# The diagonal superblock of each couple by eight block products in place of seven

## The chip, the core and the metric

The kernel runs on one core of one Trainium2 chip. The metric is the device time of one launch in microseconds; lower is better. The kernel before was run three times: 1091.76, 1091.03 and 1094.78 us, median 1091.76 us.

## What is computed

```python
scores = scale * np.matmul(z, z.transpose(0, 2, 1))      # scale = 1/S, z: (8, 3072, 64)
attn = np.maximum(scores, 0.0) ** 2
out = np.matmul(attn, v)                                 # v: (8, 3072, 256)
x = (u * out).reshape(8 * 3072, 256)
h1 = x @ w1
h2 = x @ w2                                              # w1, w2: (256, 1024)
out = np.maximum(h1, h2) @ w_out                         # w_out: (1024, 256)
```

Inputs and the output are float32; the kernel works in bfloat16 with float32 sums. The scores are symmetric, since both sides are z.

## The kernel before, in words

**Tiling.** A batch has 3072 rows: 24 tiles of 128, 6 groups of 4 tiles (512 rows), 3 couples of 2 groups. `A[b, g, blk]` is a score block of 512 keys by 512 queries, already through relu and square. It fills one of 27 SBUF slots of 128x2048 bf16. Only blocks with `blk >= g` are computed, each in two "pairs" (`score_pair`, L188): two matmuls over 64 rows (L202) into two of the four PSUM buffers of `mm_psum`, a relu on ScalarE into one of three `r_sb` buffers (L215), a square on VectorE into the slot (L223, or L221 for the blocks on the diagonal, of which the triangle alone is computed and the rest is turned over by DMA, L226). A block off the diagonal is turned by one DMA from SyncE into a second slot (`mirror`, L249, DMA at L251), which gives `A[b, blk, g]`.

**Slots.** `free` is a list; a new `Block` takes its first entry, and `release` appends. A block that is to be mirrored has two uses: the mirror is one (it releases when the DMA is issued, not when it has landed), the products are the other. A slot thus can come back into `free` as soon as a mirror is issued, and what is then written there waits until that DMA has read it.

**Couples.** Batch 0 is done by plain loops, its last couple by `plain_steps`. From batch 1 on, for each couple (b, c) the rows of A that belong to it are three superblocks of 2x2 blocks, one for each couple `o` of keys; o = c is the superblock on the diagonal. With v cut into 2x2 parts, A times v is done by seven products of blocks in place of eight (Winograd's form). It needs sums of blocks S1, S2, S3 (`prepare`, L307 to L330) and S4 (L760), each one VectorE instruction over 128x2048, and sums of parts of v (`combine_v`, L155). S1 and S2 take a slot each; S3 and S4 are written over A21 and A12.

**Two kinds of stage alternate on TensorE.** In an A stage the products of one couple are issued (L837): every step is two matmuls of 64 contraction rows, one in each half of the array, into different PSUM banks (`ORDER`, `BANK`); 84 steps for a couple. A product is done half in each lane; where it changes lane, a GpSimd no-op stands between the halves. Between the steps, at places worked out by hand, stand the 14 score pairs of later blocks, the mirrors, the adds of finished products into `h` (L742) and the DMA issues for u, z and v. In an F stage (`second`, L669) the two groups of the couple before go through the feed-forward (`ff`, L420): max(h1, h2) is done as relu(x(w1-w2)) plus x w2, so 16 matmuls of 512 columns (L425), eight relus from PSUM on ScalarE (L432), and 40 matmuls of 256 columns (L440, L448); then a copy (L456) and the DMA out from ScalarE's queue (L457). During an F stage VectorE runs a list of tasks: the four products with u ("gates", L409) of the couple just finished, and `prepared` for the couple that comes next. A hook lets six tasks of the list into the instruction stream in each `ff` (after the first and the fourth relu, and after each of the four output tiles), the rest come after both.

**When mirrors are issued in the kernel before.** `urgent` (L238) lets a mirror go at once if its block will be overwritten by S3 or S4 (g + blk odd); the others wait until the couple in whose products they are used, and are issued there when more than `KEEP` slots are free (5, from step 37 on 2).

**Where pairs are issued.** `at_step` spreads 14 pairs over an A stage; `asked` holds one back while three squares are outstanding or no slot is free.

Of the kernel before, what the change touches and what calls it, by code (L numbers as in the profile page):

```python
# [11 lines left out]
def kernel(  # L12
# [10 lines left out]
    nc = tc.nc  # L23
    fp32 = mybir.dt.float32
    bf16 = mybir.dt.bfloat16
# [10 lines left out]
    G = 4  # L36
# [6 lines left out]
    NSLOTS = 27  # L43
    AFTER = mybir.DependencyInfo(mybir.DependencyClass.Sync, mybir.DependencyReason.DATA)
    PLAIN = 4
    KEEP = 5, 2
    c2 = float((1.0 / S) * (1.0 / S))

    consts = ctx.enter_context(tc.tile_pool(name="consts", bufs=1))
# [105 lines left out]
    def combine_v(b, piece):  # L155
        w = vp[b, piece]
        b11, b12 = w[:, 0:G, 0:P], w[:, 0:G, P:D]
        b21, b22 = w[:, G : 2 * G, 0:P], w[:, G : 2 * G, P:D]
        t = tpool.tile([P, 3, G, P], bf16, name="vt")
        t1, t2, t3, t4 = vt[b, piece] = b12, t[:, 0], t[:, 1], t[:, 2]  # L160
        return [
            lambda: nc.vector.tensor_sub(t3, b22, b12),
            lambda: nc.vector.tensor_sub(t1, b12, b11),
            lambda: nc.vector.tensor_sub(t2, b22, t1),
            lambda: nc.vector.tensor_sub(t4, b21, t2),
        ]


# [66 lines left out]

        return finish

    def urgent(b, g, blk):  # L238
        return b == 0 or (g + blk) % 2

    def mirror_ready(now=None, keep=0):
        for only in (True, False):
            for x in list(to_mirror):
                if urgent(*x) if only else (x[0], x[1] // 2) == now:
                    if len(free) > (0 if only else keep):
                        to_mirror.remove(x)
                        mirror(*x)

    def mirror(b, g, blk):  # L249
        t = Block(turned=True)  # L250
# [43 lines left out]

    def alike(*blocks):
        if len({x.turned for x in blocks}) == 1:
            return [x.ap for x in blocks]
        return [  # L300
            x.ap.rearrange("p (k j r) -> p j k r", k=G, r=P)
            if x.turned
            else x.ap.rearrange("p (j k r) -> p j k r", k=G, r=P)
            for x in blocks
        ]

    def prepare(b, c):  # L307
        forms, tasks = {}, []
        for o in (c, *(o for o in range(NC) if o != c)):
            f = {  # L310
                f"A{q + 1}{k + 1}": A[b, 2 * c + q, 2 * o + k]
                for q in range(2)
                for k in range(2)
            }
            forms[o] = f

            def s1(f=f):
                f["S1"] = Block(f["A22"].turned)
                nc.vector.tensor_add(*alike(f["S1"], f["A21"], f["A22"]))  # L319

            def s2(f=f):
                f["S2"] = Block(f["A22"].turned)
                nc.vector.tensor_sub(*alike(f["S2"], f["S1"], f["A11"]))  # L323

            def s3(f=f):
                f["S3"] = f["A21"]
                nc.vector.tensor_sub(*alike(f["S3"], f["A11"], f["A21"]))  # L327

            tasks.append([s1, s2, s3])
        return forms, tasks  # L330

    ORDER = (
        (("P1", "P7", "P6", "X11"), ("P6", "X11", "P1", "P7")),
        (("X21", "X12", "P5"), ("P5", "X12b", "X21")),
    )
    BANK = {"P1": 0, "P6": 1, "P7": 2, "X11": 3, "X21": 0, "P5": 1, "X12": 2, "X12b": 3}
    PLAIN_BANK = {"D11": 0, "D12": 1, "D21": 2, "D22": 3}
    FORM = {
        "P1": ("A11", 11),
        "P6": ("S2", 1),  # L340
        "P7": ("S3", 2),
# [1 line left out]
        "P5": ("S1", 0),  # L343
        "X21": ("A22", 3),
        "X12": ("S4", 22),
        "X12b": ("S4", 22),
    }

    def product(b, c, forms, name):
        form, side = FORM[name]  # L350
        steps = []
        for o in forms:
            for j in range(G):
                if side >= 10:
                    k, dc = side // 10 - 1, side % 10 - 1
                    w = lambda o=o, j=j, k=k, dc=dc: v_at(b, (2 * o + k) * G + j, dc)
                else:
                    w = lambda o=o, j=j, side=side: vt[b, o][side][:, j, :]
                steps.append((name, w, lambda o=o, form=form: forms[o][form], j))
        return steps  # L360

    PLAIN_LANES = (("D11", "D12", "D21", "D22"), ("D21", "D22", "D11", "D12"))

# [56 lines left out]
    def ff(b, g, xT, last=False, hook=lambda *at: None):  # L420
        g_sb = gpool.tile([P, KF, GW], bf16, name="g_sb")
        for nb in range(KF):
            d_ps = mm_psum.tile([P, GW], fp32, name="d_ps", tag="mm")
            for kc in range(KD):
                nc.tensor.matmul(  # L425
                    d_ps,
                    w15_sb[:, kc, ts(nb, P)],
                    xT[:, kc, :],
                    start=(kc == 0),
                    stop=(kc == KD - 1),  # L430
                )
            nc.scalar.activation(g_sb[:, nb, :], d_ps, AF.Relu)  # L432
            hook(1, nb)
        dst = by_tile(out[ds(b * S, S), :])[:, ds(g * G, G), :]
        for t0 in range(0, G, 2):
            o_ps = mm_psum.tile([P, 2, D], fp32, name="o_ps", tag="mm")
            o_sb = opool.tile([P, 2, D], fp32, name="o_sb")
            for t in range(2):
                for dc in range(KD):
                    nc.tensor.matmul(  # L440
                        o_ps[:, t, :],
                        xT[:, dc, ts(t0 + t, P)],
                        W2o_sb[:, dc, :],
                        start=(dc == 0),
                        stop=False,
                    )
                for nb in range(KF):
                    nc.tensor.matmul(  # L448
                        o_ps[:, t, :],
                        g_sb[:, nb, ts(t0 + t, P)],  # L450
                        w_out_sb[:, nb, :],
                        start=False,
                        stop=(nb == KF - 1),
                    )
                hook(2, t0 + t)
            nc.scalar.copy(o_sb, o_ps)  # L456
            nc.scalar.dma_start(out=dst[:, ds(t0, 2), :], in_=o_sb)  # L457
# [77 lines left out]
    with tc.manual_schedule():  # L535
# [150 lines left out]
        def prepared(i, gates):  # L686

            b, c = couples[i]
            for o in range(NC):
# [2 lines left out]
                    for q in (2 * c, 2 * c + 1)  # L692
                    for k in (2 * o, 2 * o + 1)
                ), (i, done)
            for x in list(to_mirror):
                if x[0] == b and x[2] // 2 == c:
                    to_mirror.remove(x)
                    mirror(*x)
            if not b:
                return {}, list(gates)  # L700
            tasks = []
            for o in reversed(range(NC)):
                if (b, o) not in vt:
                    tasks += combine_v(b, o)
            forms, sums = prepare(b, c)
            first, *others = [x[:2] for x in sums]
            tasks = list(gates) + first + tasks + sum(others, [])
            return forms, tasks + [x[2] for x in sums]

        b, g = groups[PLAIN - 1]  # L710
        sums = drain(acc, range(KD))
# [4 lines left out]
        for i in range(PLAIN // 2, len(couples)):  # L716
# [13 lines left out]
            for f in forms.values():  # L730
                for name, n in (("A11", 1), ("A12", 2), ("A21", 1), ("A22", 1), ("S1", 1)):
                    f[name].quota = 2 * G * n
            if not b:
                for q in (q1, q2):
                    for k in range(NG):
                        A[b, q, k].quota = 4 * G
            for pair in steps:
                for x in pair:
                    left[x[0]] = left.get(x[0], 0) + 1
# [25 lines left out]
            def c11():  # L765
                add(h["1"], h["1"], h["x"])

            def after_x12():
                add(h["U2"], h["U2"], acc["X12"])
                add(h["U2"], h["U2"], acc["X12b"])  # L770

            def after_p5():
                h["V"] = new_h()
                add(h["V"], h["U3"], acc["P5"])
                add(h["U2"], h["U2"], acc["P5"])

            def after_x21():
                add(h["U3"], h["U3"], acc["X21"])

            def after_plain():  # L780
                for n, name in enumerate(("D11", "D12", "D21", "D22")):
                    h[name] = new_h()
                    copy = nc.vector.tensor_copy if n % 2 else nc.scalar.copy
                    copy(h[name], acc[name])

            events = {}
            f = list(forms.values())
            for n, do in () if not b else (
                (ends["P6"], after_p1),
                (ends["P6"], after_p6),  # L790
                (ends["P7"], after_p7),
                (ends["X11"], after_x11),
                (ends["X11"] - 7, lambda: s4(f[0])),
                (ends["X11"] - 3, lambda: s4(f[1])),
                (ends["X11"], lambda: s4(f[2])),
                (ends["X11"] + 18, c11),
                (ends["X12"], after_x12),
                (ends["P5"], after_p5),
                (ends["X21"], after_x21),
            ):  # L800
                events.setdefault(n, []).append(do)
# [15 lines left out]
                    if b or c == 2:  # L817
                        events.setdefault(n, []).append(do)

            asked = 0  # L820
            for s, pair in enumerate(steps):
                tick += 1
                flush(tick)
                mirror_ready((b, c), KEEP[s > 36])
                asked += len(at_step.get(s, ()))
                while asked and len(due) < 3 and (free or pairs[done][2] % 2):
                    emit_pair(wait=6)
                    asked -= 1
                for do in events.get(s, ()):
                    do()  # L830
                for half, (name, w, blk, j) in enumerate(pair):
# [20 lines left out]
                    a.quota -= 1  # L852
                    if not a.quota:
                        a.release()
            assert not asked, (i, asked)
            flush()
            for do in events.get(len(steps), ()):
                do()
# [47 lines left out]
```

## Time and profile before

| | |
|---|---|
| median of three runs | 1091.76 us |
| the profiled execution: its own time / its span | 1091.76 us / 1089.9 us |
| mean granted TensorE clock | 0.937 |
| busy: TensorE / VectorE / ScalarE | 966.8 / 720.1 / 612.9 us |
| DMA queue q1 (DMAs of SyncE, nearly all transposes), share of 16 engines | 48.8% |
| DMA queue q0 (loads, GpSimd) and q10 (stores) | 18.5% and 6.5% |
| A stage matmuls (L837) | 3720 |

The profile page shows one execution. "Busy" of a matmul row overlaps with its neighbours, since two halves of the array work side by side, so a mean duration there is no price of a step; the length of a stage is. The chain of work that ended last says what the end had to wait for. The table of waits says who was idle and what ended it. A table by stretches of time gives for each stretch its length, the busy time of each engine with the number of its instructions, the granted clock and the DMA share. The run is periodic from batch 1 (129.45 us) on: three A and three F stages for each batch.

### The profile page before, as it was taken

The page shows a single profiled execution, that of the slowest core. Times are in us where ns is not written, and L with a number is a line of the kernel's source. Part 1 is how long each engine was busy: PE and PEld are TensorE (multiplying, and loading weights), DVE is VectorE, ACT ScalarE, POOL GpSimd, SP SyncE. Part 2 cuts the span into 40 slices and gives each one's busy share as a digit, 9 for nine tenths or more (in the row PEclk, how much of TensorE's full clock was granted, in tenths as well). Part 3 has the DMA queues.
Part 4 walks back from the last instruction along what each step waited for, and adds up shares of the span by engine and source line. Part 5 has one row for each costly group of instructions (what it writes and reads, how often), then busy time and mean ns, then how long its engine had stood idle before and what let it go on. Part 6 is the DMA issues. An engine that isn't in the chain of part 4 may idle for free.

```text
span 1089.9 us, 19275 instructions
## 1 busy us (share of the span) xinstructions
PE 966.8 (89%) x7538; PEld 518.6 (48%) x7538; DVE 720.1 (66%) x1098; ACT 612.9 (56%) x1206; POOL 56.6 (5%) x111
## 2 busy tenths in 40 slices
PE   9989969799697996969969799697996979969998
PEld 4445525455253552535525445253552544525555
DVE  6844837679385794857938679475793867937740
ACT  7877635466464664637636476454663647644425
POOL 3000000000000000000000000000000000000000
PEclk9999978899898998989989899798998989989999
DMA  9999586956979469695686956869569795684701
GB/s 180 188 208 183 112 150 120 165 103 130 155 125 158 109 124 161 126 154 108 124 151 130 156 119 123 151 125 150 103 129 150 131 157 116 122 146 95 134 28 59
DMA packets 388652, 145.99 MB, mean 134 GB/s; under 512 B 361936, under 2 KB 365904, under 8 KB 388560
## 3 DMA queue, kind: packets, MB, share of 16 engines
q1 hardware_dynamic: 359328, 90.09, 48.8%
q0 software_dynamic: 15408, 29.50, 18.5%
q10 hardware_dynamic: 13824, 25.17, 6.5%
q8 instruction: 59, 0.97, 0.4%
q14 instruction: 33, 0.27, 0.1%
HBM read 59.77 MB, written 25.17 MB: 78 GB/s over the span
## 4 chain that ended last, share of the span: by engine, by line
PE 68%; ACT 15%; DMA 11%; DVE 2%; SPq 2%; issue 2%; ACTq 1%; DVEq 0%
PE acc L837 35%; PE o_ps L448 13%; ACT g_sb L432 12%; DMA blk<-blk 11%; PE d_ps L425 7%; PE s_ps L202 6%; PE acc L267 3%; PE o_ps L440 3%; ACT o_sb L456 1%; ACT r_sb L215 1%; DVE blk L223 1%; SPq L178 1%; SPq L251 1%; ACTq L457 1%; DVE blk L221 0%
## 5 line engine op out<-in xcount | busy, mean ns | idle before, releaser
L215 ACT ACTIVATE r_sb<-s_ps 128x512 bf16<-128x512 f32 (+3 forms) x664 | 329.4, 557 | 263.3 <-DVE blk L223 123.7
L837 PE MATMUL acc<-blk,v_sb 64*128 64x512 bf16 x2208 | 459.0, 381 | 0.0
L837 PE MATMUL acc<-blk,vt 64*128 64x512 bf16 x1512 | 373.3, 383 | 0.0
L223 DVE TENSOR_TENSOR blk<-r_sb 128x1024 bf16<-128x1024 bf16 x251 | 168.7, 688 | 172.9 <-DMA blk<-blk 104.9
L425 PE MATMUL d_ps<-xT,w_sb 128*128 128x512 bf16 x768 | 212.1, 422 | 61.1 <-ACT r_sb L215 57.5
L837 PEld LDWEIGHTS <-v_sb 64*128 64x128 bf16 x2208 | 177.9, 95 | 136.0 <-issue 7.3
L432 ACT ACTIVATE g_sb<-d_ps 128x512 bf16<-128x512 f32 x384 | 198.4, 624 | 37.5 <-PE d_ps L425 34.6
L448 PE MATMUL o_ps<-w_out_sb,g_sb 128*128 128x256 bf16 x1536 | 210.0, 274 | 6.5 <-ACT g_sb L432 5.6
L837 PEld LDWEIGHTS <-vt 64*128 64x128 bf16 x1512 | 141.3, 95 | 73.4 <-issue 8.8
L202 PE MATMUL s_ps<-zT 64*128 64x512 bf16 (+3 forms) x672 | 128.8, 361 | 49.0 <-ACT r_sb L215 47.7
L448 PEld LDWEIGHTS <-g_sb 128*128 128x128 bf16 x1536 | 151.1, 98 | 38.4 <-ACT g_sb L432 19.9
L425 PEld LDWEIGHTS <-w_sb 128*128 128x128 bf16 x768 | 78.9, 105 | 183.6 <-issue 132.2
L456 ACT COPY o_sb<-o_ps 128x512 f32<-128x512 f32 x96 | 56.2, 586 | 151.3 <-PE o_ps L448 147.1
L742 DVE TENSOR_TENSOR h_sb<-h_sb,acc 128x512 f32<-128x512 f32 x147 | 96.8, 682 | 42.6 <-ACT h_sb L746 35.4
L221 DVE TENSOR_TENSOR blk<-r_sb 128x512 bf16<-128x512 bf16 (+3 forms) x170 | 48.1, 321 | 109.2 <-DMA blk<-blk 62.7
L323 DVE TENSOR_TENSOR blk<-blk,blk 128x2048 bf16<-128x2048 bf16 x63 | 77.2, 1225 | 2.1
L319 DVE TENSOR_TENSOR blk<-blk,blk 128x2048 bf16<-128x2048 bf16 x63 | 76.7, 1217 | 2.3 <-DMA blk<-blk 2.3
L202 PEld LDWEIGHTS <-zT 64*128 64x128 bf16 x672 | 35.7, 94 | 88.8 <-issue 50.0
L761 DVE TENSOR_TENSOR blk<-blk,blk 128x2048 bf16<-128x2048 bf16 x63 | 76.5, 1217 | 0.0
L440 PE MATMUL o_ps<-W2o_sb,xT 128*128 128x256 bf16 x384 | 74.8, 277 | 0.0
L327 DVE TENSOR_TENSOR blk<-blk,blk 128x2048 bf16<-128x2048 bf16 x63 | 73.2, 1217 | 0.0
L409 DVE SCALAR_TENSOR_TENSOR xT<-h_sb,uT 128x512 bf16<-128x512 f32 x96 | 59.9, 682 | 0.0
(52 smaller groups left out, 295.9 us busy)
## 6 DMA issues: line engine op xcount, KB each, us to landing
out_dram<-o_sb ACTq DMA_DIRECT2D x96, 256.0 KB, 2.2
un<-in_u_dram POOLq DMA_DIRECT2D x48, 256.0 KB, 5.3
v_sb<-in_v_dram POOLq DMA_DIRECT2D x21, 512.0 KB, 6.3
blk<-blk SPq DMA_TRANSPOSE x246, 4.7
zn<-in_z_dram POOLq DMA_DIRECT2D x21, 128.0 KB, 3.9
v_sb<-in_v_dram POOLq DMA_DIRECT2D x6, 256.0 KB, 7.3
blk<-in_moe_w_dram POOLq DMA_DIRECT2D x2, 512.0 KB, 7.2
uT<-un SPq DMA_TRANSPOSE x48, 3.6
```

What stands on the lines that cost most here:

```text
L202: nc.tensor.matmul(s_ps[h][:, lo[h] :], zT[rows, z_at(b, blk * G + tiles[h]), :], zT[rows, q + lo[h] // P : q + G, :].rearrange("p t c -> ...
L215: nc.scalar.activation(o, s, AF.Relu)
L223: nc.vector.tensor_mul(a[:, k : k + 2, :], r, r)
L319: nc.vector.tensor_add(*alike(f["S1"], f["A21"], f["A22"]))
L323: nc.vector.tensor_sub(*alike(f["S2"], f["S1"], f["A11"]))
L425: nc.tensor.matmul(d_ps, w15_sb[:, kc, ts(nb, P)], xT[:, kc, :], start=(kc == 0), stop=(kc == KD - 1),)
L432: nc.scalar.activation(g_sb[:, nb, :], d_ps, AF.Relu)
L440: nc.tensor.matmul(o_ps[:, t, :], xT[:, dc, ts(t0 + t, P)], W2o_sb[:, dc, :], start=(dc == 0), stop=False,)
L448: nc.tensor.matmul(o_ps[:, t, :], g_sb[:, nb, ts(t0 + t, P)], w_out_sb[:, nb, :], start=False, stop=(nb == KF - 1),)
L742: nc.vector.tensor_add(out, a, b_)
L761: nc.vector.tensor_sub(f["A12"].ap, f["A12"].ap, f["S2"].ap)
L837: mm = nc.tensor.matmul(a.out(acc[name]), w()[rows], a.moving(rows, j), start=name not in opened, stop=left[name] == 0,)
```

## The change

The superblock on the diagonal is multiplied by plain products; the two others keep the seven. A couple's products are now: P1, P6, P7, P5 of 8 steps, X11, X12, X21 of 8 steps for the two superblocks off the diagonal and 8 for the own one, and a new D22 of 8: 88 steps in place of 84. The order of the products, their banks and their lanes change. S1 to S4 are formed for two superblocks, so a couple takes 4 slots for sums in place of 6. `combine_v` writes four parts into a tile of its own and is called for pieces other than the couple's own.

Mirrors go in the order in which their blocks are ready, as soon as any slot is free; `urgent`, `KEEP` and the mirrors at the head of `prepared` are gone. A pair is issued at its step, with no `asked`. In `ff`, three of the eight relus go to VectorE.

Over the whole kernel TensorE gets 3888 matmuls at L837 in place of 3720; VectorE 42 each of S1, S2, S3, S4 in place of 63, and 144 relus from PSUM; ScalarE 240 relus there in place of 384; `combine_v` stays at 84 instructions, and all loads, stores and transposes stay the same in number. The diff, cut to its core:

```diff
-        t = tpool.tile([P, 3, G, P], bf16, name="vt")
-        t1, t2, t3, t4 = vt[b, piece] = b12, t[:, 0], t[:, 1], t[:, 2]
+        t = tpool.tile([P, 4, G, P], bf16, name="vt")
...
-    def mirror_ready(now=None, keep=0):
-        for only in (True, False):
-            for x in list(to_mirror):
-                if urgent(*x) if only else (x[0], x[1] // 2) == now:
-                    if len(free) > (0 if only else keep):
-                        to_mirror.remove(x)
-                        mirror(*x)
+    def mirror_ready(keep=0):
+        while to_mirror and len(free) > keep:
+            mirror(*to_mirror.pop(0))
...
-        for o in (c, *(o for o in range(NC) if o != c)):
+        for o in range(NC):
+            if o == c:
+                continue
...
     ORDER = (
-        (("P1", "P7", "P6", "X11"), ("P6", "X11", "P1", "P7")),
-        (("X21", "X12", "P5"), ("P5", "X12b", "X21")),
+        (("P1", "P6", "P7", "X11"), ("X11", "P1", "P6", "P7")),
+        (("D22", "X12", "P5", "X21"), ("P5", "X21", "D22", "X12")),
     )
-    BANK = {"P1": 0, "P6": 1, "P7": 2, "X11": 3, "X21": 0, "P5": 1, "X12": 2, "X12b": 3}
+    BANK = {"P1": 0, "P6": 1, "P7": 2, "X11": 3, "D22": 0, "P5": 1, "X21": 2, "X12": 3}
...
+    OWN = {"X11": (0, 0), "X12": (0, 1), "X21": (1, 0), "D22": (1, 1)}
...
+        if name in OWN:
+            q, dc = OWN[name]
+            for k in range(2):
+                for j in range(G):
+                    own.append((
+                        name,
+                        lambda k=k, j=j, dc=dc: v_at(b, (2 * c + k) * G + j, dc),
+                        lambda k=k, q=q: A[b, 2 * c + q, 2 * c + k],
+                        j,
+                    ))
+        return own + off if name in ("X12", "X21") else off + own
...
-            nc.scalar.activation(g_sb[:, nb, :], d_ps, AF.Relu)
+            if nb in (2, 5, 7):
+                nc.vector.tensor_single_scalar(
+                    out=g_sb[:, nb, :], in_=d_ps, scalar=0.0, op=ALU.max
+                )
+            else:
+                nc.scalar.activation(g_sb[:, nb, :], d_ps, AF.Relu)
...
-            for x in list(to_mirror):
-                if x[0] == b and x[2] // 2 == c:
-                    to_mirror.remove(x)
-                    mirror(*x)
...
-            first, *others = [x[:2] for x in sums]
-            tasks = list(gates) + first + tasks + sum(others, [])
-            return forms, tasks + [x[2] for x in sums]
+            return forms, list(gates) + sums[:3] + tasks + sums[3:]
...
-                (ends["P6"], after_p1),
+                (ends["P1"], after_p1),
                 (ends["P6"], after_p6),
+                (ends["P6"] + 2, lambda: s4(f[0])),
                 (ends["P7"], after_p7),
                 (ends["X11"], after_x11),
-                (ends["X11"] - 7, lambda: s4(f[0])),
-                (ends["X11"] - 3, lambda: s4(f[1])),
-                (ends["X11"], lambda: s4(f[2])),
-                (ends["X11"] + 18, c11),
+                (ends["X11"] + 3, lambda: s4(f[1])),
+                (ends["X11"] + 7, c11),
+                (ends["D22"], after_d22),
+                (ends["P5"], after_p5),
                 (ends["X12"], after_x12),
-                (ends["P5"], after_p5),
                 (ends["X21"], after_x21),
...
-            asked = 0
             for s, pair in enumerate(steps):
                 tick += 1
                 flush(tick)
-                mirror_ready((b, c), KEEP[s > 36])
-                asked += len(at_step.get(s, ()))
-                while asked and len(due) < 3 and (free or pairs[done][2] % 2):
+                mirror_ready()
+                for _ in at_step.get(s, ()):
                     emit_pair(wait=6)
-                    asked -= 1
```

## The prediction, made before the changed kernel was run

> **What bounds the kernel now.** I read the chain of waits first, for what the end hangs on, then the table by stretches, for which stages are long, then the waits, for what makes them long, and last one such place in the timeline. The chain of the page:
>
> ```profile
> PE 68%; ACT 15%; DMA 11%; DVE 2%; SPq 2%; issue 2%; ACTq 1%; DVEq 0%
> ```
>
> TensorE carries it, but 11% is a DMA from slot to slot: a mirror. The table by stretches for batch 4 (start:end, length, busy PE, PEld, DVE, ACT, POOL, then clock, DMA share, GB/s), six stages A, F, A, F, A, F; the fifth and sixth are the third couple's:
>
> ```profile
> 537.64:567.97 30.33, 23.06 (x197) 10.54 (x197) 14.28 (x23) 14.13 (x29) 1.59 (x3) 0.90 0.71 126
> 567.97:589.05 21.08, 18.49 (x114) 11.24 (x114) 18.64 (x23) 11.11 (x21) 0.53 (x1) 0.91 0.60 126
> 589.05:609.67 20.62, 20.62 (x198) 10.49 (x197) 11.79 (x26) 12.70 (x29) 1.59 (x3) 1.00 0.98 154
> 609.67:634.58 24.91, 18.10 (x114) 11.04 (x112) 19.20 (x27) 11.10 (x21) 1.05 (x2) 0.86 1.00 164
> 634.58:655.84 21.26, 21.26 (x197) 9.48 (x197) 14.72 (x22) 16.49 (x31) 1.58 (x3) 1.00 0.54 103
> 655.84:672.74 16.90, 16.58 (x116) 10.69 (x114) 16.49 (x27) 9.81 (x19) 0.01 (x1) 1.00 0.69 136
> ```
>
> The last two are what a stage costs when nothing is missing: TensorE is busy throughout and the clock is 1.00. The first, second and fourth do the same matmuls in 9.1, 4.2 and 8.0 us more, TensorE idle for a part of it and at a lower clock. The waits name the cause (who waited on whom: us, times, longest):
>
> ```profile
> ACT r_sb L215 <- DVE blk L223: 123.7, 33, 9.2
> DVE blk L223 <- DMA blk<-blk: 104.9, 14, 9.6
> DVE blk L221 <- DMA blk<-blk: 62.7, 6, 11.9
> PE d_ps L425 <- ACT r_sb L215: 57.5, 13, 8.4
> PE s_ps L202 <- ACT r_sb L215: 47.7, 7, 7.4
> ```
>
> Bottom to top it is one chain: the square that writes a score block stands on VectorE until a mirror has read the slot; the three `r_sb` buffers fill; ScalarE stops; the PSUM buffers fill; TensorE stops, 20 times (14 + 6 squares wait, 13 + 7 stalls). The timeline of batch 4 shows one:
>
> ```profile
> 558.40 9.20 SPq L251 DMA_TRANSPOSE blk<-blk  x3
> 562.97 1.29 DVE L223 TENSOR_TENSOR blk<-r_sb 128x1024 bf16<-128x1024 bf16 x2 [9.52 <-DMA blk<-blk]
> 564.41 1.07 PE L202 MATMUL s_ps<-zT 64*128 64x512 bf16 x2 [7.27 <-ACT r_sb L215]
> ```
>
> **What the stalls cost.** Stages of all seven batches against the clean ones: first couple's A, 30.15, 29.76, 29.69, 30.33, 29.56, 30.42, 29.24, together 209.2, against 7 x 21.26: 60.3 us. The F behind it, 22.24, 20.89, 19.58, 21.08, 22.31, 20.89, 23.24, together 150.2, against 7 x 16.89: 32.0. The F behind the second couple's A in six batches, 25.05, 26.64, 27.91, 24.91, 27.18, 24.50, together 156.2, against 6 x 16.89: 54.9. Sum **147.2 us**. Of it 57.5 + 47.7 = 105.2 is TensorE's idle time; the other 42, some 2.1 for each stall, is work at a low clock right after, as a shorter stretch shows (same columns, clock 0.50):
>
> ```profile
> 564.00:568.00 4.00, 3.59 (x15) 1.12 (x15) 0.27 (x1) 1.82 (x4) 0.00 (x0) 0.50 1.15 208
> ```
>
> The Trainium skill (TensorE: Matmul & The Clock Gate, "What's actually happening") says that an idle window of about 3.4 us halves the clock until a busy one has passed; half of 3.4 is 1.7 a stall, 34 us for 20, so by that rule the sum would be 8 us smaller than by the rows.
>
> **Do the stalls go?** In before, a block with two uses whose products are done is released by its mirror; five mirrors are issued in steps 42 to 49 of the first couple's A, and the next blocks (steps 48 and 60) take just those slots. Followed through both programs as built: in before exactly 20 VectorE squares wait for a mirror issued 19, 26 or 40 matmuls earlier. In the changed one mirrors go one at a time, about 12 steps apart, while their blocks are still needed, so slots come free from the products or from S4 (on VectorE itself); no VectorE or ScalarE instruction of a stage stands within 90 matmuls of a mirror that it waits for. Two slots fewer for sums pay for the earlier mirrors. So all 20 go: **-147.2**, with an uncertainty that the rivals carry. Next in line is then TensorE's own work.
>
> **More products.** 4 steps more in each of 21 couples, 84 steps (168 matmuls). The clean A stage of 21.26 us has 84 steps and 14 score pairs: 98 places, 0.217 us each. 84 x 0.217 = **+18.2**, on the path in every A; nothing hides it, for TensorE is busy there throughout.
>
> **VectorE's sums.** 84 instructions of 128x2048 at 1.22 us (rows L319, L323, L327, L761), 102 us, leave VectorE. They lay beside TensorE's work; nothing by itself.
>
> **Three relus of eight.** 144 leave ScalarE (row L432, 0.624 us) and cost VectorE the row L213's 0.684, 98.5 us in all. A clean F has 2 x (16 x 0.223 + 40 x 0.109) = 15.9 us of matmuls (the chain has 16 of L425 in 3.57 us, 8 of L448 in 0.87), so about 1.0 of 16.9 is the wait for the last relus: the most that can be won is 1.0 x 24 F stages = 24 us. But VectorE is in order and 16.49 of 16.90 us busy in a clean F. Ahead of the last relu of the second `ff` now stand: two adds of the A stage 1.4, four gates (L409, 0.682) 2.7, S1 to S3 3.65, one task more 0.43 to 1.22, six relus 4.1: 12.3 to 13.1 us. TensorE wants it 8.6 (first `ff`) + 16 x 0.223 + 10 x 0.109 = 13.2 us in. So the relus arrive about in time; in the first `ff` adds, gates and relus (1.4 + 1.4 + 2.1 = 4.9, from about 0.4) end at 5.3, no better than ScalarE's 4.7 to 5.1 now. I take a fifth of the possible gain, **-5**. If all tasks had to end within F, VectorE would need 1.4 + 2.7 + 7.3 + 8 x 0.425 + 4.1 = 18.9 us, 2.0 more: +48. Ends kept: -24 and +48. A rule of the skill speaks against this edit (VectorE: DVE Perf Modes, "Specifications"): VectorE sits closer to SBUF, ScalarE to PSUM. The rows agree mildly, 0.684 against 0.597 (L215) and 0.624 (L432); by them the move adds 144 x 0.06 to 0.09, some 9 to 13 us, of busy time, which is not the path as long as F keeps its length.
>
> **Moved steps.** S2 and S3 of the second superblock end up after all other tasks: in the longest F (eight `combine_v`) VectorE ends about 19.5 us in, and step 12 of the next A, which needs it, is at 16.5 + 14 x 0.217 = 19.5. Banks are taken over after 8 steps (1.7 us) where it was 12: X21 needs the add of P7 (0.68, behind one square 0.69 and one S4 1.22) and X12 the copy of X11 (0.59, behind up to two relus, 1.2). Between 0 and 0.3 us a couple; I take 0.15 x 21, **+3**. The relays stand in GpSimd's queue behind the same loads as before. The transposes of u (steps 42, 48) now have three mirrors ahead of them in SyncE's queue in the third couple's A, which had at most one. q1's 48.8% is 532 us for 90.09 MB, so a mirror of 0.524 MB takes 3.1 us of all engines: 3 x 3.1, two halves for u, and loads of 7 (q0: 202 us for 29.5 MB, 1 MB here) make 19.5; the gates want u at about 23. Nothing.
>
> **Sum.** 1091.8 (the profiled execution's own time, 1.9 over its span, and equal to the median) - 147.2 + 18.2 - 5 + 3 = **961 us**.
>
> **Rivals.** *VectorE paces F*: the tasks and relus together bind, +48 in place of -5: 1014 us. For it: 16.49 of 16.90. Against: only part of the tasks stands ahead of a relu. *Half the stalls stay*, because mirrors that run on through every stage bring q1 late and something waits that I counted as free: 961 + 74 = 1035. For it: DMA time of 73.8% of 1090 us is 84% of 961, and the third couple's A has seven mirrors where three were issued. Against: no waiting instruction is near its mirror. *Slower*: in the third couple's A the transposes of u come so late that the first gate waits in F; a relu stands behind it on VectorE, TensorE behind that, and the clock falls. It decides when u is over 4 us late (23 - 19.5), and to pass 1091.8 it has to take 131 us, 18.7 in each of 7 batches or 5.5 in each F: such as 1110 us. Against: the clean A stage at 589.05 us carries a DMA share of 0.98 without a stall. *No effect*: the same count of stalls and relus that win back the 18 us: about 1092; the order as built speaks against it.
>
> **Chances.** 961 with all its terms (940 to 985) 0.74; VectorE paces F (985 to 1015) 0.12; half the stalls stay 0.07; slower 0.05; no change 0.02. The range takes the first two with the relus' ends: 935 (all of 24 won, 961 - 19, and a little) to 1012. A measurement tells 0.3% from no change: faster by more 0.93, within 0.02, slower 0.05.
>
> **What would show it.** Right: no line "DVE blk <- DMA blk<-blk" of any size; granted clock near 1.00; all A stages of 21.5 to 22.2 us, all F of 16 to 17.5. Wrong: an F over 18 with relus behind S tasks (first rival); a gate waiting on "DMA uT<-un" (slower); squares that wait for a mirror (half the stalls).

## The result and the profile after

The changed kernel takes **946.39 us** (median of four runs, 943.65 to 954.8; the kernel before beside it 1093.27, 1091.03 to 1096.02): a ratio of 0.867, 95% interval 0.861 to 0.873. 961 had been predicted, with a range of 935 to 1012. (In experiments 1, 6, 10 and 11 one of the four executions was over 1.5% longer than the fastest, at a lower clock; the medians here are of all four, the ratios and intervals leave that one out.) The profiled execution took 945.2 us, its span 943.4; the mean granted clock rose from 0.937 to 0.996.

The chain of work that ended last, on the page of the kernel after:

```profile
PE 91%; DVE 5%; ACT 1%; issue 1%; DMA 1%; SPq 0%; ACTq 0%; DVEq 0%
```

The 11% that hung on a DMA are 1%, ScalarE's 15% are 1%: what is left is TensorE's own work. The table by stretches: the first two lines are the third couple's A and the F behind it in batch 4, the next four those of the first and the second couple in batch 5 (columns as before: length, busy PE, PEld, DVE, ACT, POOL, clock, DMA share, GB/s):

```profile
548.61:570.73 22.12, 22.12 (x205) 9.85 (x204) 14.78 (x22) 16.69 (x31) 2.10 (x4) 1.00 1.04 185
570.73:586.87 16.14, 16.08 (x114) 10.72 (x113) 15.20 (x25) 7.19 (x13) 0.02 (x1) 1.00 0.97 188
586.87:608.67 21.80, 21.80 (x205) 10.42 (x205) 16.98 (x29) 15.57 (x31) 2.12 (x4) 1.00 0.68 117
608.67:624.82 16.15, 16.09 (x115) 10.74 (x114) 15.20 (x23) 7.19 (x13) 0.00 (x0) 1.00 0.95 179
624.82:646.30 21.48, 21.48 (x206) 11.00 (x205) 15.97 (x35) 14.28 (x31) 1.58 (x3) 1.00 1.01 143
646.30:662.53 16.23, 16.08 (x115) 10.72 (x114) 15.01 (x21) 7.19 (x13) 0.53 (x1) 1.00 1.01 160
```

TensorE's busy time equals the length in every A, and misses it by 0.06 to 0.15 us in every F; no clock is below 1.00. The DMA engines are at 0.68 to 1.04 of their time, and TensorE waits for none of them. In the table of waits a single square still stands on a mirror, for 0.4 us, where 20 did for 167.6. The one mirror that holds somebody up for longer is in the first F of the run, with the stall it makes on TensorE:

```profile
ACT o_sb L456 <- DMA blk<-blk: 6.1, 1, 6.1
...
PE d_ps L420 <- ACT o_sb L456: 3.9, 1, 3.9
...
DVE blk L222 <- DMA blk<-blk: 0.4, 1, 0.4
```

TensorE's waits fell from 118.5 us in all to 9.0.

### The profile page after: what moved, and what is told of

Read it like the earlier page. It is cut to its first block, busy times and chain, and to the rows that moved or that the text cites. A ratio compares the mean times of both kernels' runs of the same rounds, so it can differ in the third digit from the quotient of the medians.

```text
span 943.4 us, 19492 instructions
## 1 busy us (share of the span) xinstructions
PE 929.3 (99%) x7706; PEld 517.5 (55%) x7706; DVE 717.3 (76%) x1158; ACT 552.8 (59%) x1062; POOL 57.0 (6%) x111
## 4 chain that ended last, share of the span: by engine, by line
PE 91%; DVE 5%; ACT 1%; issue 1%; DMA 1%; SPq 0%; ACTq 0%; DVEq 0%
PE acc L829 44%; PE o_ps L448 16%; PE d_ps L420 15%; PE s_ps L201 7%; PE o_ps L440 4%; PE acc L259 4%; DVE xT L404 1%; DVE g_sb L428 1%; ACT r_sb L214 1%; DMA blk<-blk 1%; DVE h_sb L735 1%; DVE blk L311 1%; DVE blk L303 0%; DVE blk L307 0%; DVE blk L222 0%
## 5 line engine op out<-in xcount | busy, mean ns | idle before, releaser
L829 PE MATMUL acc<-blk,v_sb 64*128 64x512 bf16 x2544 | 467.1, 376 | 0.0
L829 PE MATMUL acc<-blk,vt 64*128 64x512 bf16 x1344 | 328.6, 376 | 0.0
L829 PEld LDWEIGHTS <-v_sb 64*128 64x128 bf16 x2544 | 183.7, 94 | 141.5 <-issue 4.6
L448 PE MATMUL o_ps<-w_out_sb,g_sb 128*128 128x256 bf16 x1536 | 202.9, 273 | 1.2 <-DVE g_sb L428 0.4
L420 PE MATMUL d_ps<-xT,w_sb 128*128 128x512 bf16 x768 | 180.3, 382 | 5.2 <-ACT o_sb L456 3.9
L829 PEld LDWEIGHTS <-vt 64*128 64x128 bf16 x1344 | 125.6, 94 | 70.7
L432 ACT ACTIVATE g_sb<-d_ps 128x512 bf16<-128x512 f32 x240 | 130.3, 599 | 56.8 <-PE d_ps L420 52.3
L420 PEld LDWEIGHTS <-w_sb 128*128 128x128 bf16 x768 | 73.4, 98 | 100.7 <-issue 24.7
L428 DVE TENSOR_SCALAR g_sb<-d_ps 128x512 bf16<-128x512 f32 x144 | 96.2, 685 | 42.6 <-PE d_ps L420 34.2
L259 PE MATMUL acc<-blk,v_sb 64*128 64x512 bf16 x384 | 50.6, 376 | 1.8 <-DVE blk L222 1.3
L311 DVE TENSOR_TENSOR blk<-blk,blk 128x2048 bf16<-128x2048 bf16 x42 | 51.4, 1223 | 1.2
L754 DVE TENSOR_TENSOR blk<-blk,blk 128x2048 bf16<-128x2048 bf16 x42 | 51.1, 1218 | 0.0
```

What stands on the lines that cost most here:

```text
L259: nc.tensor.matmul(a.out(acc[half, dc]), v_at(b, t, dc)[rows], a.moving(rows, j), start=first, stop=last,)
L420: nc.tensor.matmul(d_ps, w15_sb[:, kc, ts(nb, P)], xT[:, kc, :], start=(kc == 0), stop=(kc == KD - 1),)
L428: nc.vector.tensor_single_scalar(out=g_sb[:, nb, :], in_=d_ps, scalar=0.0, op=ALU.max)
L448: nc.tensor.matmul(o_ps[:, t, :], g_sb[:, nb, ts(t0 + t, P)], w_out_sb[:, nb, :], start=False, stop=(nb == KF - 1),)
L829: mm = nc.tensor.matmul(a.out(acc[name]), w()[rows], a.moving(rows, j), start=name not in opened, stop=left[name] == 0,)
```

## The experiments

The prediction held that slot reuse alone makes the 20 stalls, and that mirrors issued early and one by one take them away: the *slot theory*. Two rivals of that are taken up here: that the stalls go because VectorE has less to do, and that the mirrors' place in SyncE's queue does the harm. The change has three parts that can be had apart: the **products** (eight for the own superblock, four sums, the new order, and with it the score pairs at their steps), the **mirrors** (at once), the **relus** (three of eight on VectorE). Where a median of four runs is given, an interval stands with it; the others are single executions. Stage lengths for a kind of stage are means over batches 1 to 6, where nothing else is said.

### 1. After, with all relus on ScalarE

```diff
-            if nb in (2, 5, 7):
-                nc.vector.tensor_single_scalar(out=g_sb[:, nb, :], in_=d_ps, scalar=0.0, op=ALU.max)
-            else:
-                nc.scalar.activation(g_sb[:, nb, :], d_ps, AF.Relu)
+            nc.scalar.activation(g_sb[:, nb, :], d_ps, AF.Relu)
```

> The changed kernel with all eight relus of the feed-forward back on ScalarE, nothing else. Theory: the move is worth what the clean F stages show, 16.9 us before against 16.14 after, 0.75 us in each of 24 F stages, so about 945 + 18 = 963 us, the A stages unchanged (21.8, 21.5, 22.1). Rival one, the prediction's own small share: 945 + 5 = 950. Rival two, the F stages became shorter for another reason (a shorter task list on VectorE): 945, no change.

963.11 us (962.48 to 978.78), ratio to before 0.881 [0.877, 0.885]. The A stages stay as in the kernel after (21.80, 21.48, 22.12), and nearly every F is 16.89 in place of 16.13 to 16.23; the third couple's F of batch 4:

```profile
578.98:595.87 16.89, 16.46 (x113) 10.70 (x114) 13.85 (x21) 9.81 (x19) 0.02 (x1) 1.00 0.91 176
```

The relus are worth 963.1 - 946.4 = 16.7 us (17.4 between the two profiled executions), all in F, and in these two kernels they have nothing to do with the stalls.

### 2. After, with the late mirrors of before

```diff
+    def urgent(b, g, blk):
+        return b == 0 or (g + blk) % 2
...
-                mirror_ready()
+                mirror_ready((b, c), KEEP[s > 36])
```

> The changed kernel with the mirror rule of before (urgent blocks at once, the others in the couple that uses them, KEEP). As built, 13 squares then stand 62 to 64 matmuls behind a mirror that they wait for (19 to 40 in the kernel before, where there were 20). Theory of the slots: stalls come back, smaller, 0 to 6 us for each of 13, so 950 to 1020 us, with waits of the form DVE blk <- DMA blk<-blk in the trace. Rival, the products and their order made the difference: 945, no such wait.

1000.25 us. The waits of squares for mirrors are back, 14 of them:

```profile
DVE blk L221 <- DMA blk<-blk: 43.6, 6, 8.3
DVE blk L223 <- DMA blk<-blk: 36.9, 8, 7.9
```

The first and second couple's A take 24.16 and 25.13 us in place of 21.80 and 21.48 (the first couple's 33.53 in batch 1 and 21.80 to 23.07 in the others), and the F behind them 17.6 and 17.8 in place of 16.2. So the mirrors' times are needed for the whole of the gain, as the slot theory says; but no more than 54 of the 147 us came back.

### 3. Before, with three relus on VectorE

The edit of experiment 1 the other way round, in the kernel before.

> The kernel before with three of eight relus on VectorE, nothing else. Theory: the 20 stalls stay, the clean F stages win 0.75 us each, so 1075 to 1092 us. Rival, ScalarE's load was what made the stalls: under 1000.

1172.48 us, 79 more than before (1093.2, run beside it); both theories missed. The loss is in the three kinds of stage that already stalled: the first couple's A 29.98 to 34.50, its F 21.16 to 24.53, the F behind the second couple's A 26.03 to 29.35, together 6 x 11.2 = 67 us in batches 1 to 6. The clean A stages are unchanged (20.62, 21.26), the clean F 16.89 to 17.17. The squares' waits for mirrors are longer, 185.3 us (109.9 + 75.4) in 21 waits where it was 167.6 in 20. The same edit wins 17 us in the kernel after. The timelines show how the loss comes about: with the relus VectorE ends the couple's sums 8.8 us into the first couple's A (584.5 - 575.66), where it was 3.9 (541.5 - 537.64), and so the squares and the transposes behind them come later, the mirrors with them:

```profile
600.57 9.38 SPq L251 DMA_TRANSPOSE blk<-blk  x3
```

That is 24.9 us into the stage, where the same three mirrors stood 20.8 us in before (558.40 - 537.64).

### 4. Before, with rested slots

A slot that a mirror has released is not taken again within 84 steps as long as another is free; nothing else is changed. It takes away what the slot theory blames.

```diff
+            cool = [n for n, a in enumerate(free) if tick - resting.get(id(a), -999) > REST]
-            self.ap = free.pop(0)
+            self.ap = free.pop(cool[0] if cool else 0)
```

> The kernel before with one change: a slot that a mirror released is not taken again within 84 steps while another slot is free. Seven products everywhere, late mirrors and relus as before. As built, no square stands near a mirror that it waits for. Theory: the 147 us of stalls go and nothing else changes, so about 945 us, clock near 1.00, with A stages of 20.6 to 21.3 and F of 16.9. Rival one, the bursts of mirrors delay others (the transposes of u behind five mirrors, then a gate): 960 to 1010. Rival two, the diagonal superblock's sums or the seven products are the cause: over 1050.

1078.24 us (1070.04 to 1084.97), ratio 0.986 [0.980, 0.992]. The slot theory in its narrow form fell. The first couple's A and F are clean (20.94 and 16.89 us; 25.09 for the A of batch 1), as it had said; but the second couple's A went from 20.62 to 26.73 and the F behind it from 26.03 to 31.30. The time lies where the second rival put it, over 1050, but its cause (the sums, the seven products) is not what the waits name, and experiments 6 and 10 come to 1000 and 990 with both in place. The waits name two new victims of the same mirrors:

```profile
DVE xT L414 <- DMA uT<-un: 139.3, 19, 13.2
...
ACT o_sb L461 <- DMA blk<-blk: 65.0, 7, 11.7
```

SyncE's queue shows the first (start, length, then the instructions):

```profile
557.71 1.77 SPq L183 DMA_TRANSPOSE uT<-un  x1
559.57 10.69 SPq L256 DMA_TRANSPOSE blk<-blk  x3
570.36 1.69 SPq L183 DMA_TRANSPOSE uT<-un  x1
```

Three mirrors hold the queue for 10.7 us, and the second transpose of u stands behind them; the gate that needs it waits 11.0 us on VectorE. This is the mechanism of the prediction's rival "slower", in another kernel. The theory that I put in its place: the *burst* of late mirrors does harm in more than one way, and where one is closed it takes the next.

### 5. Before, with the mirrors at once

```diff
-                if urgent(*x) if only else (x[0], x[1] // 2) == now:
-                    if len(free) > (0 if only else keep):
+                if only:
+                    if len(free) > 0:
```

> The kernel before with the mirror rule of the changed one (in the order in which the blocks are ready, as soon as a slot is free); seven products on all three superblocks, relus on ScalarE and the held-back pairs stay. Theory, revised after the run with rested slots: late mirrors issued in one burst are the cause, by two ways, the slots they release and the transposes of u queued behind them; both go here, so the time falls by most of 147 us, to 945 to 975 (pairs are held back to steps 28 to 54 for want of slots, which may cost some us in each A). Rival: two superblocks' sums more on VectorE (102 us) or the slots they take keep it slow: over 1030.

991.37 us (985.53 to 994.68), ratio 0.908 [0.903, 0.912], between the two. No square waits for a mirror, and the clock is 0.997. But the three A stages are 23.01, 22.71 and 22.21 where a clean one is 20.94, 20.62 and 21.26, and the F behind the second couple's A is 18.62. In the program as built the 27 slots run out with six of them taken by sums, and `asked` holds the score pairs back: in a first or second couple's A two go at steps 2 and 7, none until step 32, and seven from there to step 48. TensorE then waits for a buffer once in each of these 13 stages:

```profile
PE s_ps L202 <- ACT r_sb L215: 15.0, 13, 1.2
```

That is 15.0 of the 27 us that the first and second couples' A lose; how the rest comes about is not shown.

### 6. Rested slots, and u earlier

Experiment 4 with the transposes of u at steps 30 and 36 in place of 42 and 48, ahead of the burst.

> The run with rested slots, and the transposes of u moved from steps 42 and 48 to 30 and 36, ahead of the burst of mirrors in SyncE's queue. Theory: the gates no longer wait for u (139 us of waits of VectorE in that run), VectorE's sums and the z transposes behind them are in time, and what was left of the stalls goes: 945 to 970. Rival, it is the burst's load on the DMA engines and not the place in the queue: over 1030, with waits of other instructions for DMAs.

999.05 us (995.06 to 1012.81), ratio 0.914 [0.909, 0.919]. (The waits are those of an execution of 1012.81 us.) Two gates still wait for u, 10.8 us together, where 19 waited 139.3. What TensorE still waits for is ScalarE's copy of the output, which waits for a mirror, 73.7 us in 6 waits: the second victim of experiment 4.

### 7. Mirrors at once, with three relus on VectorE

Experiments 5 and 3 together: the change without its products.

> The kernel before with mirrors at once and three of eight relus on VectorE. Theory: 18 us below the same without the relus' move, 927 to 955, and then below the changed kernel, since 84 steps (18 us) are saved. Rival, three superblocks' sums and the relus are too much for VectorE in F, so the relus come late there: F stages over 17 us and a time above that of mirrors at once alone.

1024.57 us (1019.04 to 1033.06), ratio 0.941 [0.936, 0.946]: 33 more than experiment 5, as the rival had it. Here the prediction's first rival, VectorE paces F, is what happens, but its price stands mostly in the next A:

```profile
PE acc L842 <- DVE blk L323: 19.1, 14, 1.6
...
PE o_ps L453 <- DVE g_sb L433: 10.0, 42, 0.3
```

TensorE waits for relus in F (42 times, 10.0 us) and, in the first couple's A alone, for sums that come late (14 times, 19.1 us). That A takes 27.37 us in place of 23.01, 4.4 more in each batch; the F stages are 17.4 to 18.2 us, where they were 16.89 to 18.62.

### 8. Before, with u earlier alone

> The kernel before with the transposes of u at steps 30 and 36 in place of 42 and 48, nothing else. Theory of two ways: the 20 squares still wait for their slots, so most stalls stay, 1060 to 1095. Rival, the queue is the only way: under 1000.

1119.86 us, 28 more than before, outside of what both expected. The squares wait longer for the mirrors, 111.2 + 93.2 = 204.4 us in 20 waits in place of 167.6; the clean A stages are unchanged. The transposes of u now stand ahead of mirrors which the squares wait for; whether that is the whole of the 28 us I did not settle. It shows at any rate that in the kernel before neither of these two orders of SyncE's queue is free.

### 9. The products alone

After, with the edits of experiments 1 and 2.

> The changed kernel with the late mirrors and all relus on ScalarE: of the change only the products are left (plain diagonal superblock, two superblocks' sums, pairs issued at their steps). With it all eight combinations of products, mirrors and relus but one have been run. As built 13 squares stand 62 to 64 matmuls behind a mirror. Theory: a lighter VectorE and later reuse of slots make most stalls small, as with late mirrors and relus on VectorE (1000), plus up to 18 for F at 16.9: 1000 to 1020 us. Rival: the products alone change nothing but their 18 us: 1090 to 1110.

1000.12 us, 90 less than before, with 14 squares that wait for mirrors (43.2 + 34.3 us). The stalls that remain sit in the second couple's A (24.96 for 21.48) and the F behind it (18.93 for 16.89). The products cost 18 us of TensorE, so they took away some 108 us of stalls with the mirror rule of before. But the same rule gives other times here: with two slots fewer in sums more slots are free, and as built two of the first couple's mirrors go ahead of its first step and two at step 37, where these four went at steps 42 to 46. SyncE's queue shows the second two:

```profile
508.13 5.51 SPq L251 DMA_TRANSPOSE blk<-blk  x2
```

The stage starts at 496.91: 11.2 us in, where three mirrors stood 20.8 us in before. So a part of this gain is that of earlier mirrors.

### 10. Rested slots, u earlier, and the late mirrors apart

Experiment 6, and a mirror that is not urgent is issued 8 steps or more after the last: the burst without the burst.

```diff
+                if urgent(*x) if only else (x[0], x[1] // 2) == now and tick >= late[0]:
+                        if not only:
+                            late[0] = tick + 8
```

> The kernel before with rested slots, the transposes of u at steps 30 and 36, and late mirrors at least 8 steps apart in place of a burst. Theory: what was left with the first two of these was the store on ScalarE's queue waiting for a mirror of the burst; spread, it goes too, all A stages are 20.6 to 21.3 and all F stages 16.9, and the time is 940 to 960 us. Rival: SyncE's queue is behind for good in the second couple's A, so the F behind it stays at 20 to 30 us: 980 to 1000.

989.81 us (985.23 to 1005.36), ratio 0.908 [0.905, 0.911]; 940 to 960 had been the theory. That is the rival's time, and the stage that it named. Five of the six kinds of stage are clean: 20.94, 16.89, 20.62, 21.26, 16.93. The sixth, the F behind the second couple's A, takes 23.87, 7.0 too much, 42 us in six batches, and 989.8 - 42 = 948. It is the copy on ScalarE (the table of waits, then the timeline of one):

```profile
ACT o_sb L464 <- DMA blk<-blk: 53.3, 7, 8.9
```

```profile
566.77 0.37 ACTq L465 DMA_DIRECT2D out_dram<-o_sb  x1
567.23 0.58 ACT L464 COPY o_sb<-o_ps 128x512 f32<-128x512 f32 x1 [8.03 <-DMA blk<-blk]
```

A copy and a store have nothing to do with a mirror; no buffer is shared. In the program as built the store's issue waits on the semaphore of a transpose eight DMAs back in the order of SyncE's and ScalarE's queues, since those semaphores are used in turn. ScalarE stands there for 8 us with the next `ff`'s relus behind the store, and TensorE behind those (5.81 us). The rival's cause has its part in this: the second couple's late mirrors, in the program at steps 44, 49 and 52, stand together in SyncE's queue when that couple's A ends (552.49), so here the burst was not thinned:

```profile
552.08 12.71 SPq L259 DMA_TRANSPOSE blk<-blk  x3
```

The third of them is issued at 562.23 and lands at 566.69, and the store goes at 566.77. How much of the 42 us is the late queue and how much the shared semaphore, no run separates.

### 11 and 12. One relu on VectorE

Experiment 10 and the kernel after, each with `nb == 5` alone on VectorE.

> The same with the sixth of the eight relus on VectorE. Theory: with the diagonal's sums still on VectorE one relu is what it can take; F stages of 16.2 to 16.7, so 5 to 15 us below the same without it, 928 to 955 us and perhaps below the changed kernel. Rival, as with three relus in the kernel before: VectorE late in F, 10 to 30 us above.

> The changed kernel with one relu of eight on VectorE (the sixth) in place of three. Theory: ScalarE with seven relus ends them about when TensorE wants the last, so most of the 0.75 us of each F stays won: 946 to 952 us. Rival, the gain is in proportion to the relus moved: 957.

With the old products 1015.99 us (1011.94 to 1027.93; 0.931 [0.927, 0.935]), 26 more than experiment 10, as the rival had it; some 20 of it are in the first couple's A, 23.84 for 20.94 in six of seven batches. With the new ones 947.94 (946.44 to 950.59; 0.870 [0.868, 0.872]), the same as the kernel after: one relu wins what three do. No version that was run is faster than the change.

### The three parts together

Medians, less that of the kernel before run beside each; a star marks a single execution:

| | relus on ScalarE | three on VectorE | the relus |
|---|---|---|---|
| before | 0 | +79* | +79* |
| mirrors at once | -100 | -67 | +33 |
| products | -90* | -93* | about 0 |
| products, mirrors at once | -130 | -147 | -17 |

None of the parts has a price of its own. Products or mirrors alone win 90 and 100; together they win 130 and not 190, because both take away the same stalls; and the same three relus cost 79 us or win 17, going by what else VectorE has to do.

## Why the prediction was right, point by point

**The stalls, -147.2.** All 20 went, as the order in the built programs had told. Their size was nearly right: I took 21.26 us for the first couple's clean A, the third couple's length; experiment 10 shows it as 20.94, so they cost 209.2 - 7 x 20.94 = 62.6 in that stage in place of 60.3, in all 149.5. The clock records of before side with the rows in the 42 us put down to the low clock: they show 136.5 us at clock 0.50, with TensorE busy for 87.9 of them, and work at half the pace for that long costs 44. By the estimate from the page's rule that the prediction weighed (the Trainium skill, TensorE: Matmul & The Clock Gate, "What's actually happening") the sum would have been 8 us smaller.

The reason that I gave was too narrow. Slot reuse is what the trace of before shows; but without it (experiment 4) only 15 us are won. The late mirrors do harm in three ways: by the slots they release, by the transposes of u behind them in SyncE's queue, and by a store on ScalarE that waits for their semaphore. A trace shows the one that comes first. Experiments 4, 6 and 10 close two of them and thin the burst in part, and come to 990. In the change the mirrors go singly, and no instruction of a stage stands near one that it waits for, so all three end but for the first F. That takes both parts: with the mirrors at once and the old products (experiment 5) the slots run out, with the new products and late mirrors (experiments 2 and 9) 14 squares wait. That so narrow a reason gave the right number is in part luck: the change closes ways that it does not name. The same reason, with 945 us forecast, missed experiment 4 by 133.

**The products, +18.2.** A stages grew from 20.94, 20.62 and 21.26 to 21.80, 21.48 and 22.12: 0.86 us each, 18.1 in 21 couples.

**VectorE's sums, "nothing by itself".** True of the path, and yet the step that carries the relus. Without their going three relus cost 33 us (experiment 7), with it they win 17; and the products alone take away most stalls under the late mirrors' rule. Whether that is the 102 us fewer on VectorE or the two slots fewer for sums, no run here separates; the mirrors that go earlier in experiment 9 give the slots a share.

**The relus, -5: the term that was mis-sized.** They won 16.7. For the first `ff` I let VectorE's instructions follow each other by their durations, 0.682 to 0.684 us. They do not. VectorE's timeline in the F at 570.73 of the kernel after:

```profile
571.05 1.28 DVE L735 TENSOR_TENSOR h_sb<-h_sb,acc 128x512 f32<-128x512 f32 x2
572.25 0.68 DVE L404 SCALAR_TENSOR_TENSOR xT<-h_sb,uT 128x512 bf16<-128x512 f32 x1
572.85 0.68 DVE L428 TENSOR_SCALAR g_sb<-d_ps 128x512 bf16<-128x512 f32 x1
573.45 0.68 DVE L404 SCALAR_TENSOR_TENSOR xT<-h_sb,uT 128x512 bf16<-128x512 f32 x1
574.05 1.28 DVE L428 TENSOR_SCALAR g_sb<-d_ps 128x512 bf16<-128x512 f32 x2
...
580.35 0.69 DVE L428 TENSOR_SCALAR g_sb<-d_ps 128x512 bf16<-128x512 f32 x1 [0.29 <-PE d_ps L420]
...
582.61 0.69 DVE L428 TENSOR_SCALAR g_sb<-d_ps 128x512 bf16<-128x512 f32 x1 [0.17 <-PE d_ps L420]
```

Each takes 0.68 us, and the next starts 0.60 after it; two together take 1.28. The relus of the first `ff` end 4.6 us into the F (574.05 + 1.28 - 570.73), where I had sized 5.3 and ScalarE's 4.7 to 5.1. So the first `ff` loses nothing, where by my sum it would have lost most of what the second wins, and the gain stands in the second: it begins 8.05 us into the F where it was 8.12, so 0.07 of the 0.75 us is won ahead of it and the rest in it. There it is VectorE that waits for TensorE, as the sum of 12.3 to 13.1 us against 13.2 allowed. The F went to 16.15 on the mean of 18 stages, 0.74 below 16.89, and is near the 15.9 us of its matmuls. That one relu wins as much (experiment 12) says the same: what counts is that ScalarE is relieved and VectorE not late.

**New waits, +3.** None is seen: the A stages are longer by the steps added and no more.

**The sum.** 1091.8 - 149.5 + 18.1 - 16.7 = 943.7; measured 945.2. The rest of 1.5 is more than covered by the first F, 23.19 us where it was 20.94: ScalarE's store waits there for a mirror too, as the kernel after's timeline shows,

```profile
79.79 0.59 ACT L456 COPY o_sb<-o_ps 128x512 f32<-128x512 f32 x1 [6.08 <-DMA blk<-blk]
80.42 1.01 PE L420 MATMUL d_ps<-xT,w_sb 128*128 128x512 bf16 x2 [3.86 <-ACT o_sb L456]
```

**The rivals.** "VectorE paces F" is real, in experiment 7, though most of its price falls in A; the lighter products keep it away. "Half the stalls stay" came with late mirrors (experiment 2), not, as I had put it, with a busy q1: the DMA share is 1.04 in an A without a stall. "Slower" by a late u: its wait came in experiment 4 (139.3 us), not its price, for that kernel is still below before.

## What to carry to other kernels

A wait in the table names the first victim of a late transfer, not all of them: before a stall is put down to what is waiting, ask what else stands behind the same transfer (in its queue, on its semaphores), for there the time goes when the first way is closed. Parts of a change that share a cause or an engine have no prices of their own: the same three relus were worth -17 to +79 us here, by the slack of the engine that took them. And what an in-order engine can deliver is read from the distance of the starts in its timeline, not from the sum of durations.

## What the runs showed of the hardware that was not expected

- VectorE instructions of 128x512 with a float32 or PSUM operand take 0.68 us and start 0.60 us apart when nothing holds the next. The Trainium skill (Vector Engine (DVE) Microarchitecture Reference, "Measured stream behaviour on trn2") gives 1.0417 ns for a column and some 75 ns for an instruction after queue overlap, measured on integer streams; from these an estimate is 512 x 1.0417 + 75 = 608 ns, which agrees with the distance of starts, not with the duration.
- A store on ScalarE's queue waited 8.03 us for a transpose of SyncE's queue with which it shares no data (experiment 10, 53.3 us in 7 waits); in the kernels before and after this is one wait each, of 1.9 and 6.1 us.
- DMA engines at a share of 0.95 to 1.04 of a stage did TensorE no harm here, where nobody needed a transfer soon: five of the six stages shown are there in the kernel after, at a clock of 1.00 and with TensorE busy throughout.
